# A change to the order of loads, conversions and first instructions in the attention stage of a fused attention, SwiGLU and top-1-expert kernel

## The chip, the cores and the metric

The kernel runs on one core of one Trainium2 chip. The metric is device time in microseconds (us) of one launch. Engines are named as in the profile: PE is TensorE's matmuls, PEld its weight loads, DVE is VectorE, ACT is ScalarE, POOL is GpSimd, SP is SyncE, which issues nearly all DMAs here. Each engine works through its own instructions in a fixed order and waits at any whose input or buffer isn't ready.

## What is computed

The reference, cut to its core (B=2, H=8, S=768, D=64; then 1536 tokens of 512, two feed-forward layers):

```python
scores = q @ k.T / 8 - slope[h] * dist      # local window n_local or first n_global keys, else -1e9
a = softmax(scores);  x = (a @ v) as [1536, 512]
xn = x / sqrt(mean(x*x) + 1e-6) * rms_g
x = (silu(xn @ w_gate) * (xn @ w_val)) @ w_out          # 1536 hidden columns, weights in float64
e = argmax(x @ r_gate);  out = gate * (relu(x @ w1[e]) @ w2[e])   # 8 experts
```

The SwiGLU weights arrive as float64, so each block of them is loaded raw (512 KB) and converted on the chip to a pair of rounded parts, high and low. Matmuls outside the first half of attention take such pairs too (high times high, high times low, low times high).

## The kernel before, in words

Attention is cut into 6 stages of 256 tokens and 4 pairs of heads: 24 groups g0 to g23, each with 2 units of 128 queries, so units u0 to u47. Groups 0 to 7 (`NRAWG = 8`) multiply queries and keys as they come. From g8 on, keys and queries are split into rounded parts first: ACT writes the high part of the keys (L519), DVE the low one (L522), then ACT and DVE do the same for the queries (L531, L532), and POOL copies pieces (L446). A unit is: scores on PE (L572 for raw groups, L586 for split ones), table added and row maximum on DVE (L590), exponential on ACT (L594), transposes on PE (L605), their copy on ACT (L613), values on PE (L634), and after a group's second unit a division on DVE (L641 to L643). After a stage's last group come its norm (L412 to L418) and four transposes per 128 tokens, whose result ACT and DVE take out of PSUM as a pair (L428, L429). From then on the first SwiGLU sweep of that stage (L801, L809 to L819, L838, L847) can run between the units.

SP loads keys, queries and values of a group in `load_pair`. Keys of group g are asked for when group g-2 is prepared, queries and values one group ahead. There are three key buffers and two query buffers (`NKN, NQN = 3, 2`), so a load also waits until the group that had the buffer has read it. A raw weight block goes through `load64` (L344) into one of three raw buffers (`NRAW = 3`), and `convert64` turns it into a pair: absolute value on ACT (L358), clamp, shift, sign and low bits on DVE (L361, L364, L367, L370), high part on ACT (L377), low part on DVE for the first four blocks and on POOL after that (L378).

The program is written in one order and a scheduler, which reckons each instruction's time, sets the final order on each engine. A helper, `behind(i, first)`, asks that instruction `i` stand behind `first` in that order; it adds no semaphore. The body counts events in `nun` (one at the start, one for each unit, one for each finished stage), and gives out the nine conversions of the first sweep (gate and value blocks 0, 1, 2, then three output blocks) by a list:

```python
    PREPS = [2, 4, 6, 8, 20, 22, 24, 27, 30]
            pin["load"] = key_load.get(10) if nun >= 12 else None
            while preps and nun > PREPS[9 - len(preps)]:
                preps.pop(0)()
```

`pin["load"]` is what a raw block's load must stand behind on SP: the key load of g10, once 12 events have passed. `pin["act"]` is the last exponential written so far, and a conversion's first ACT instruction stands behind it.

Before the body, the kernel reads `n_global` and `n_local`, makes tables from them on DVE and POOL (L275 to L292), halves them on ACT (L297), and works out a flag (L124 to L131) that every engine reads to choose between the fast and the dense body (L310, L1378). PE runs 24 dummy matmuls (`WARM0`, L181) ahead of its reading of the flag, 12 more at the body's start and two with each of the first 16 units.

Of the kernel before, what the change touches and what calls it, by code (L numbers as in the profile page):

```python
# [8 lines left out]
F32 = mybir.dt.float32  # L9
# [4 lines left out]
ACTF = mybir.ActivationFunctionType  # L14
ALU = mybir.AluOpType
# [4 lines left out]
P = 128  # L20
# [4 lines left out]
NP = H // 2  # L25
# [20 lines left out]
def kernel(  # L46
# [16 lines left out]
    nc = tc.nc  # L63
    slope = [2.0 ** (-(h + 1)) for h in range(H)]
# [11 lines left out]
    NDV = 512  # L76
    HP = 0
    NRAW = 3
    PREPS = [2, 4, 6, 8, 20, 22, 24, 27, 30]
    NA = 3  # L80
    MMA = "mm mm mm s s"
    MMB = "mm mm mm s s"
# [14 lines left out]
    TAILSEQ = "rrxrxxr"  # L97
    WARM3 = 6
    TAIL, TOFF = [0]*6, 0
    WARM0, WARM1, WARM2, WARMU = 24, 12, (2,), 16  # L100

    const = ctx.enter_context(tc.tile_pool(name="const", bufs=1))
    dram = ctx.enter_context(tc.tile_pool(name="dram", bufs=1, space=DRAM))
# [15 lines left out]
        out=nval, in0=nneg, scalar=4294967296.0, in1=nf[:, :, 0], op0=ALU.mult, op1=ALU.add  # L119
    )  # L120
    ng, nl = nval[:, 0:1], nval[:, 1:2]
# [6 lines left out]
    )  # L128
    nc.vector.tensor_tensor(out=flagf[:, 3:4], in0=flagf[:, 0:1], in1=flagf[:, 2:3], op=ALU.mult)
    flag = const.tile([1, 1], I32, name="flag")  # L130
    nc.vector.tensor_copy(flag, flagf[:, 3:4])  # L131


    gB = const.tile([P, DM], F32, name="gB")
# [16 lines left out]

    mhalf = const.tile([P, ST_MAX], F32, name="mhalf")
    nc.vector.memset(mhalf, -0.5)

    wz = const.tile([P, P], BF16, name="wz")
    nc.vector.memset(wz, 0.0)
# [12 lines left out]
    def behind(i, first):  # L169

        tc.add_manual_dep(
            i.ins, first.ins.name,
            mybir.DependencyInfo(mybir.DependencyClass.NoSync, mybir.DependencyReason.DATA), reason="order",
        )
# [26 lines left out]
    def is_raw(st, hp):  # L201
        return st * NP + hp < NRAWG

    last_load, key_load = [None], {}

    def load_pair(st, hp, kn, qn, vn, what="kqv"):
        b, t0, nt = STARTS[st] // TB, STARTS[st] % TB, SIZES[st]
        i0 = 0 if t0 else 1
        nk = nt + 1 - i0
        k0 = (t0 - 1 + i0) * P  # L210
        hd = slice(P * hp, P * (hp + 1))
        if is_raw(st, hp):
            if "k" in what:
                last_load[0] = nc.sync.dma_start(out=kn[:, 0:nk * P], in_=kT[b][hd, k0:k0 + nk * P])
            if "q" in what:
                nc.sync.dma_start(out=qn[:, 0:nt * P], in_=qT[b][hd, t0 * P:(t0 + nt) * P])
        else:
            for c, x, src in (("k", kn, kT[b][hd, k0:k0 + nk * P]), ("q", qn, qT[b][hd, t0 * P:(t0 + nt) * P])):
                if c not in what:
                    continue  # L220
                for r in range(2):
                    i = nc.sync.dma_start(
                        out=x[D * r:D * (r + 1), 0:2 * src.shape[1]].rearrange("d (j s) -> d j s", j=2),
                        in_=src.rearrange("(j d) s -> d j s", j=2),
                    )
                if c == "k":
                    last_load[0] = key_load[st * NP + hp] = i
        if "v" in what:
            nc.sync.dma_start(
                out=rows_of(vn)[:, i0:i0 + nk, 1:P + 1],  # L230
                in_=v[b, k0:k0 + nk * P, hd].rearrange("(t p) c -> p t c", p=P),
            )
        return kn, qn, vn
# [38 lines left out]
    tabG = const.tile([P, 256], F32, name="tabG")  # L272
    tab0 = const.tile([P, P], F32, name="tab0")
    gcol = const.tile([P, GW], F32, name="gcol")
    nc.vector.tensor_scalar(out=keep, in0=rel, scalar1=nl, scalar2=None, op0=ALU.is_lt)  # L275
    nc.vector.scalar_tensor_tensor(out=keep, in0=rel, scalar=0.0, in1=keep, op0=ALU.is_ge, op1=ALU.mult)
    nc.vector.tensor_tensor(out=rel, in0=rel, in1=keep, op=ALU.mult)
    nc.vector.tensor_scalar(out=keep, in0=keep, scalar1=-MASK, scalar2=MASK, op0=ALU.mult, op1=ALU.add)
# [33 lines left out]
    def body(is_fast):  # L312
# [122 lines left out]
        def fast_attention(pool):  # L435
# [12 lines left out]
            def prep(gi):  # L448
# [64 lines left out]
                src = kn[:, 0:2 * nk * P].rearrange("p (j t n) -> p j t n", j=2, t=nk)  # L513
                ks = kt[:, :, OW + i0:OW + nt + 1, :]
                hi_dve = HI[gi >= HIN]
                if hi_dve[0]:
                    nc.vector.tensor_copy(ks, src)
                else:
                    nc.scalar.activation(out=ks, in_=src, func=ACTF.Copy)  # L519
                lo_eng = (nc.vector, nc.gpsimd)  # L520
                kq = KQ0 if gi < KQN else KQ
                lo_eng[kq[0]].tensor_tensor(out=ks[D:P], in0=src[D:P], in1=ks[D:P].bitcast(F32), op=ALU.subtract)  # L522
# [3 lines left out]
                if hi_dve[1]:  # L526
                    nc.vector.tensor_scalar(
                        out=qhi, in0=srq, scalar1=0.125 / slope[2 * hp], scalar2=None, op0=ALU.mult
                    )
                else:  # L530
                    nc.scalar.activation(out=qhi, in_=srq, func=ACTF.Copy, scale=0.125 / slope[2 * hp])  # L531
                lo_eng[kq[1]].scalar_tensor_tensor(  # L532
                    out=qt[:, :, 1, 0:n], in0=srq, scalar=0.125 / slope[2 * hp], in1=qhi.bitcast(F32),
                    op0=ALU.mult, op1=ALU.subtract,
# [9 lines left out]
            units = [(g, t) for g in range(len(order)) for t in range(SIZES[order[g][0]])]  # L544

            def scores(g, t):
                st, t0, hp, qt, kt, vn, vx, mx = groups[g]
                if not is_raw(st, hp):
                    sb = ps("s", NS, "sp")
                    sp = [sb[:, 0:256], sb[:, 256:512]]  # L550
                else:
                    un = units.index((g, t))
                    mmb = is_raw(st, hp) and un % 2
                    sp = [ps(*(("mm", NMM) if mmb else ("s", NS)), "sp") for _ in range(2)]
                first = t0 + t == 0
                plain = t0 + t == 1
                n = P if first else 256
                tab = tabs[0 if first else 1 if plain else 2]
                pr = pool.tile([P, 2, 256], F32, tag="pr", bufs=NPR, name="pr")
                OW = ST_MAX  # L560
                raw_ = is_raw(st, hp)
                if raw_:
                    kn, kgr_ = kt
                    mm = warm(WARM2[un % len(WARM2)], into=sp) if un < WARMU else None
                    rows = [slice(D * j, D * (j + 1)) for j in range(2)]
                    if t0 == 0:
                        parts = [((0, n), kn[:, 0:n])]
                    else:
                        parts = [((0, GW), kgr_[:, hp, :]), ((GW, n), kn[:, t * P + GW:(t + 2) * P])]
                    for (c0, c1), keys in parts:  # L570
                        for o, r in zip(sp, rows):
                            last_, mm = mm, nc.tensor.matmul(  # L572
                                out=o[:, c0:c1], lhsT=qt[r, t * P:(t + 1) * P], rhs=keys[r], start=True, stop=True
                            )
                            if last_ is not None:
                                behind(mm, last_)
                for j, a in () if raw_ else ((0, 0), (0, 1), (1, 0), (1, 1)):
                    o = sp[j][:, 0:n]
                    if first:
                        rhs = kt[:, j, OW + 1, :]  # L580
                    elif plain:
                        rhs = kt[:, j, OW + t:OW + t + 2, :].rearrange("p t n -> p (t n)")
                    else:
                        rhs = kt[:, j, t:t + OW + 2:OW + 1, :]
                        o = o.rearrange("p (a n) -> p a n", a=2)
                    mm = nc.tensor.matmul(  # L586
                        out=o, lhsT=qt[:, j, a, t * P:(t + 1) * P], rhs=rhs, start=(a == 0), stop=(a == 1)
                    )
                for j in range(2):
                    nc.vector.tensor_tensor_reduce(  # L590
                        out=pr[:, j, 0:n], in0=sp[j][:, 0:n], in1=tab[j][:, 0:n], scale=-slope[2 * hp],
                        scalar=3.0e38, op0=ALU.add, op1=ALU.min, accum_out=mx[:, t, j:j + 1],
                    )
                    pin["act"] = nc.scalar.activation(  # L594
                        out=pr[:, j, 0:n], in_=pr[:, j, 0:n], func=ACTF.Exp, bias=mx[:, t, j:j + 1],
                        scale=-1.0,
                    )
                return pr, n
# [597 lines left out]
        nun = 0  # L1196
# [5 lines left out]
        while True:  # L1202
            with tc.high_priority(HP):
                ev = next(att, None)
            if ev is None:
                break
            if isinstance(ev, tuple):
                ready.append(ev[1])
            nun += 1
            if is_fast and nun == LATE:  # L1210
                late_loads()
            pin["load"] = key_load.get(10) if nun >= 12 else None
            while preps and nun > PREPS[9 - len(preps)]:
                preps.pop(0)()
            credit += MOE_RATE
            while True:
                if moe is None and ready:
                    st = ready.pop(0)
                    moe = moe_block(0, range(M0[st]), st, mpool, False)
                    credit = 0.0  # L1220
                if moe is None or credit <= 0:
                    break
                c = next(moe, None)
                if c is None:
                    moe = None
                    done += 1
                else:
                    credit -= c
# [197 lines left out]
```

## Time and profile before

| what | us |
|---|---|
| median of 3 runs | 648.56 |
| lowest, highest of them | 645.32, 649.33 |
| the profiled execution | 643.62 |
| its span, first to last instruction | 641.9 |
| around the span | 1.72 |

The span is what the trace shows; rows below are of that one execution, in us from its start. "Granted clock" is the share of TensorE's full clock (2.4 GHz) that the chip granted; 0.50 is the lower of its two levels, 1.2 GHz. In rows by stretch the columns are the stretch, its length, then busy us (and number of instructions) of PE, PEld, DVE, ACT and POOL, the granted clock, the share of the DMA engines and GB/s. Bracketed numbers in a row of the timeline are the engine's idle time just before, and what ended it.

### The profile page before, as it was taken

The page shows a single profiled execution, that of the slowest core. Times are in us where ns is not written, and L with a number is a line of the kernel's source. Part 1 is how long each engine was busy: PE and PEld are TensorE (multiplying, and loading weights), DVE is VectorE, ACT ScalarE, POOL GpSimd, SP SyncE. Part 2 cuts the span into 40 slices and gives each one's busy share as a digit, 9 for nine tenths or more (in the row PEclk, how much of TensorE's full clock was granted, in tenths as well). Part 3 has the DMA queues.
Part 4 walks back from the last instruction along what each step waited for, and adds up shares of the span by engine and source line. Part 5 has one row for each costly group of instructions (what it writes and reads, how often), then busy time and mean ns, then how long its engine had stood idle before and what let it go on. Part 6 is the DMA issues. An engine that isn't in the chain of part 4 may idle for free. (4 is left out here: it accounts for less than half of the span.)

```text
span 641.9 us, 11652 instructions
## 1 busy us (share of the span) xinstructions
PE 623.2 (97%) x4280; PEld 560.2 (87%) x4281; DVE 446.6 (70%) x1096; ACT 317.4 (49%) x623; POOL 179.5 (28%) x255
## 2 busy tenths in 40 slices
PE   8988989999999999999999999999999999999995
PEld 3667979999999999999999999997788998998994
DVE  3967989896599997775359998953576656556520
ACT  2867957797455543335522221242566556455420
POOL 4323434353121321221222533461701211011011
PEclk9998969999999999999999999999999999999998
DMA  7567556540044442221411020343777658465000
GB/s 220 150 188 182 168 158 186 154 98 28 1 117 146 132 138 93 66 67 66 132 66 66 1 67 34 89 159 100 272 259 249 222 206 266 148 227 181 5 29 32
DMA packets 56567, 82.98 MB, mean 129 GB/s; under 512 B 7983, under 2 KB 38703, under 8 KB 56496
## 3 DMA queue, kind: packets, MB, share of 16 engines
q1 hardware_dynamic: 53552, 74.75, 38.2%
q0 software_dynamic: 2944, 7.35, 3.4%
q8 instruction: 37, 0.61, 0.4%
q14 instruction: 34, 0.28, 0.1%
HBM read 75.75 MB, written 7.39 MB: 130 GB/s over the span
## 5 line engine op out<-in xcount | busy, mean ns | idle before, releaser
L801 PE MATMUL pg<-xn,gv 128*128 128x256 f32 x1728 | 226.2, 284 | 0.2 <-DVE hf L814 0.2
L801 PEld LDWEIGHTS pg<-xn,gv 128*128 128x128 f32 x1728 | 219.0, 190 | 7.0 <-DVE hf L814 0.7
L838 PE MATMUL po<-ow,hid 128*128 128x512 f32 x432 | 114.9, 398 | 0.1
L819 POOL TENSOR_TENSOR hid<-hf,hid 128x256 fp32r<-128x256 f32 x72 | 63.1, 878 | 166.6 <-ACT hid L818 166.5
L1049 PE MATMUL py<-ew,eh 128*128 128x512 f32 x384 | 91.1, 395 | 0.8 <-DVE eh L1116 0.4
L838 PEld LDWEIGHTS po<-ow,hid 128*128 128x128 f32 x432 | 76.1, 189 | 12.4 <-DVE hf L814 0.3
L1049 PEld LDWEIGHTS py<-ew,eh 128*128 128x128 f32 x384 | 71.3, 188 | 17.5 <-DVE eh L1116 0.8
L1071 PE MATMUL ph<-xs,ew 128*128 128x256 f32 x672 | 83.0, 283 | 0.0
L1071 PEld LDWEIGHTS ph<-xs,ew 128*128 128x128 f32 x672 | 81.6, 190 | 0.7
L818 ACT ACTIVATE hid<-hf 128x256 fp32r<-128x256 f32 x72 | 29.9, 415 | 84.9 <-DVE hf L814 84.9
L870 DVE CUSTOM_DVE_ANT_0 jk<-duo,rgb 128x512 bf16<-128x512 f32 x64 | 54.3, 848 | 0.5
L989 DVE TENSOR_TENSOR ew<-rawe,ew 128x1024 fp32r<-128x1024 f32 (+1 forms) x36 | 40.7, 1134 | 13.2 <-ACT ew L985 13.2
L1080 DVE SCALAR_TENSOR_TENSOR eh<-ph,eh 128x256 fp32r<-128x256 f32 x56 | 23.1, 422 | 37.3 <-ACT eh L1079 37.3
L809 ACT ACTIVATE th<-pg 128x256 f32<-128x256 f32 x72 | 27.2, 380 | 44.0 <-PE pg L801 41.6
L304 POOL DMA_INDIRECT out_dram<-yo,tk x14 | 14.6, 1040 | 120.3 <-ACT yo L1057 92.6
L989 DVE TENSOR_TENSOR ew<-duo,ew 128x1024 fp32r<-128x1024 f32 x28 | 34.1, 1223 | 17.9 <-ACT ew L985 17.0
L594 ACT ACTIVATE pr<-pr,mx 128x256 f32<-128x256 f32 (+1 forms) x96 | 41.9, 484 | 9.3 <-DVE mx L590 9.1
L985 ACT ACTIVATE ew<-rawe 128x1024 fp32r<-128x1024 f32 x36 | 38.0, 1060 | 10.5 <-PE pg L801 4.7
L810 DVE SCALAR_TENSOR_TENSOR th<-th,pg 128x256 f32<-128x256 f32 x72 | 29.6, 413 | 15.5 <-ACT th L809 15.3
L1079 ACT ACTIVATE eh<-ph 128x256 fp32r<-128x256 f32 x56 | 21.2, 385 | 38.8 <-PE ph L1071 38.7
L985 ACT ACTIVATE ew<-duo 128x1024 fp32r<-128x1024 f32 x28 | 29.4, 1060 | 19.4 <-PE py L1049 19.4
L847 DVE TENSOR_TENSOR duo<-duo,po 128x512 f32<-128x512 f32 x36 | 23.3, 681 | 22.2 <-PE po L838 22.1
(183 smaller groups left out, 890.0 us busy)
## 6 DMA issues: line engine op xcount, KB each, us to landing
rawe<-in_moe_w_dram SPq DMA_DIRECT2D x36, 512.0 KB, 4.6
duo<-in_moe_w_dram SPq DMA_DIRECT2D x28, 512.0 KB, 4.3
raw<-in_moe_w_gate_dram SPq DMA_DIRECT2D x12, 512.0 KB, 4.4
raw<-in_moe_w_val_dram SPq DMA_DIRECT2D x12, 512.0 KB, 4.3
raw<-in_moe_w_out_dram SPq DMA_DIRECT2D x12, 512.0 KB, 3.6
kn<-in_k_dram SPq DMA_DIRECT2D x28, 192.0 KB, 3.5
qn<-in_q_dram SPq DMA_DIRECT2D x36, 128.0 KB, 3.2
vn<-in_v_dram SPq DMA_DIRECT2D x16, 192.0 KB, 3.1
```

What stands on the lines that cost most here:

```text
L594: pin["act"] = nc.scalar.activation(out=pr[:, j, 0:n], in_=pr[:, j, 0:n], func=ACTF.Exp, bias=mx[:, t, j:j + 1], scale=-1.0,)
L801: nc.tensor.matmul(out=pg[:, 0:n_], lhsT=gv[:, i, a, kk, :], rhs=x[st][:, kk, :], start=(n == 0), stop=(n == 3 * KD - 1),)
L809: pin["th"] = nc.scalar.activation(out=th, in_=pss[0][:, 0:n_], func=ACTF.Tanh, scale=0.5)
L810: nc.vector.scalar_tensor_tensor(out=th, in0=th, scalar=1.0, in1=pss[0][:, 0:n_], op0=ALU.add, op1=ALU.mult)
L818: nc.scalar.activation(out=hh[:, 0], in_=hf, func=ACTF.Copy)
L819: nc.gpsimd.tensor_tensor(out=hh[:, 1], in0=hf, in1=hh[:, 0].bitcast(F32), op=ALU.subtract)
L838: nc.tensor.matmul(out=po, lhsT=hid[mi][:, a, t * P:(t + 1) * P], rhs=ow[:, c, :], start=(mi == 0 and n == 0), stop=(mi == len(ms) - 1 and ...
L870: nc.vector.tensor_tensor_reduce(out=jk, in0=part[i0 + t], in1=rgb[e // 4][:, e % 4, :], scale=1.0, scalar=0.0, op0=ALU.mult, op1=ALU.add, ...
L985: cp = nc.scalar.activation(out=t[:, 0], in_=raw, func=ACTF.Copy)
L989: nc.vector.tensor_tensor(out=t[:, 1, 0:nd], in0=raw[:, 0:nd], in1=t[:, 0, 0:nd].bitcast(F32), op=ALU.subtract)
L1049: last_mm["py"] = nc.tensor.matmul(out=py, lhsT=hid(m, a, j), rhs=w2t[m // 2][:, c, (m % 2) * DM:(m % 2 + 1) * DM], start=(n == 0), stop=( ...
L1071: nc.tensor.matmul(out=ph[:, 0:CAP], lhsT=w1t[kk][:, a, m * P:(m + 1) * P], rhs=x[:, kk, :], start=(n == 0), stop=(n == 3 * KD - 1),)
```

## The change

- The conversions of gate block 2, value block 2 and output block 0 are given out at events 14, 16 and 18 in place of 20, 22 and 24; those of output blocks 1 and 2 at 26 and 29 in place of 27 and 30.
- Raw weight loads from event 12 on must stand behind the query load of g7, in place of the key load of g10. The key load of g10 must stand behind the query load of g8.
- For g8 and g9 the ACT instructions that write the high parts of keys and queries must stand behind the last exponential of the unit before (`late`, `pin["prev"]`).
- The first table instruction on DVE (L275) must stand behind the flag.
- A one-column exponential is put near the program's start on ACT. `WARM0` goes from 24 to 20.

```diff
-    PREPS = [2, 4, 6, 8, 20, 22, 24, 27, 30]
+    PREPS = [2, 4, 6, 8, 14, 16, 18, 26, 29]
-    WARM0, WARM1, WARM2, WARMU = 24, 12, (2,), 16
+    WARM0, WARM1, WARM2, WARMU = 20, 12, (2,), 16
-    nc.vector.tensor_copy(flag, flagf[:, 3:4])
+    flagged = nc.vector.tensor_copy(flag, flagf[:, 3:4])
+    first_exp = const.tile([P, 1], F32, name="first_exp")
+    nc.scalar.activation(out=first_exp, in_=mhalf[:, 0:1], func=ACTF.Exp)
-    last_load, key_load = [None], {}
+    last_load, key_load, q_load = [None], {}, {}
@@ load_pair
-                nc.sync.dma_start(out=qn[:, 0:nt * P], in_=qT[b][hd, t0 * P:(t0 + nt) * P])
+                q_load[st * NP + hp] = nc.sync.dma_start(out=qn[:, 0:nt * P], in_=qT[b][hd, t0 * P:(t0 + nt) * P])
                 for r in range(2):
+                    g = st * NP + hp
                     i = nc.sync.dma_start(
                         out=x[D * r:D * (r + 1), 0:2 * src.shape[1]].rearrange("d (j s) -> d j s", j=2),
                         in_=src.rearrange("(j d) s -> d j s", j=2),
                     )
+                    if c == "k" and 10 <= g <= 10:
+                        behind(i, q_load[g - 2])
                 if c == "k":
                     last_load[0] = key_load[st * NP + hp] = i
+                else:
+                    q_load[st * NP + hp] = i
@@ tables
-    nc.vector.tensor_scalar(out=keep, in0=rel, scalar1=nl, scalar2=None, op0=ALU.is_lt)
+    behind(nc.vector.tensor_scalar(out=keep, in0=rel, scalar1=nl, scalar2=None, op0=ALU.is_lt), flagged)
@@ prep
+                def late(i):
+                    if gi < 10:
+                        behind(i, pin["prev"])
-                    nc.scalar.activation(out=ks, in_=src, func=ACTF.Copy)
+                    late(nc.scalar.activation(out=ks, in_=src, func=ACTF.Copy))
-                    nc.scalar.activation(out=qhi, in_=srq, func=ACTF.Copy, scale=0.125 / slope[2 * hp])
+                    late(nc.scalar.activation(out=qhi, in_=srq, func=ACTF.Copy, scale=0.125 / slope[2 * hp]))
@@ scores
+                pin["prev"] = pin["act"]
@@ body's loop
-            pin["load"] = key_load.get(10) if nun >= 12 else None
+            pin["load"] = q_load.get(7) if nun >= 12 else None
```

## Rows read from the trace of the kernel before

**Rows 1.** Busy time of each engine, granted clock and DMA, by stretch.
```profile
44.00:60.00 16.00, 11.46 (x74) 10.37 (x75) 11.24 (x35) 10.44 (x24) 5.56 (x13) 0.79 0.90 219
46.90:53.70 6.80, 4.86 (x22) 4.24 (x21) 4.99 (x18) 3.49 (x8) 1.01 (x2) 0.50 1.11 234
60.00:84.00 24.00, 22.28 (x190) 21.60 (x188) 23.56 (x65) 19.86 (x45) 11.41 (x21) 1.00 0.61 177
80.00:96.00 16.00, 13.44 (x70) 12.34 (x70) 13.19 (x39) 9.19 (x21) 5.78 (x11) 0.68 0.58 159
84.40:94.70 10.30, 9.67 (x42) 9.18 (x43) 8.01 (x24) 6.70 (x16) 3.17 (x5) 0.50 0.42 120
...
160.00:641.90 481.90, 473.11 (x3196) 433.01 (x3194) 320.69 (x686) 203.44 (x371) 117.94 (x117) 1.00 0.37 121
```

**Rows 2.** What SP issues around g7 to g10, in order of time.
```profile
32.36 0.54 SPq L216 DMA_DIRECT2D qn<-in_q_dram  x1
...
37.51 2.93 SPq L222 DMA_DIRECT2D kn<-in_k_dram  x4
40.49 0.60 SPq L344 DMA_DIRECT2D raw<-in_moe_w_gate_dram  x1
...
41.68 1.26 SPq L222 DMA_DIRECT2D qn<-in_q_dram  x2
42.98 0.59 SPq L344 DMA_DIRECT2D raw<-in_moe_w_out_dram  x1
```

**Rows 3.** DMA issues of 40 to 44 us: KB each, us from issue to landing.
```profile
raw<-in_moe_w_gate_dram SPq DMA_DIRECT2D x1, 512.0 KB, 4.8
...
raw<-in_moe_w_out_dram SPq DMA_DIRECT2D x1, 512.0 KB, 8.3
...
qn<-in_q_dram SPq DMA_DIRECT2D x2, 128.0 KB, 6.9
```

**Rows 4.** The timeline around the first loss: start, us, engine, line.
```profile
39.19 0.89 ACT L594 ACTIVATE pr<-pr,mx 128x256 f32<-128x256 f32 x2
...
42.74 0.84 ACT L519 ACTIVATE kt<-kn 128x768 fp32r<-128x768 f32 x1 [2.66 <-DMA kn<-in_k_dram]
...
49.28 0.63 ACT L531 ACTIVATE qt<-qn 128x512 fp32r<-128x512 f32 x1 [2.08 <-DMA qn<-in_q_dram]
...
50.05 2.28 PE L586 MATMUL sp<-kt,qt 128*128 128x256 f32 x8 [1.43 <-ACT qt L531]
```

**Rows 5.** The conversions' instructions up to 160 us: ns min/median/max, first and last start.
```profile
L361 DVE TENSOR_SCALAR cv<-cv x11: 394/421/1324, 18.1 to 108.3; 128x512 f32<-128x512 f32 x11
L364 DVE TENSOR_SCALAR cv<-cv x11: 410/427/628, 18.6 to 108.8; 128x512 uint32<-128x512 uint32 x11
L367 DVE SCALAR_TENSOR_TENSOR cv<-raw,cv x11: 675/689/1649, 19.3 to 109.4; 128x512 uint32<-128x512 uint32 x11
L370 DVE SCALAR_TENSOR_TENSOR cv<-raw,cv x11: 679/694/1686, 20.8 to 113.4; 128x512 uint32<-128x512 uint32 x11
...
L378 POOL TENSOR_TENSOR gv<-cv,gv x2: 1272/1282/1292, 72.7 to 78.2; 128x512 fp32r<-128x512 f32 x2
```

**Rows 6.** The timeline around the second loss, and the conversion before it.
```profile
63.98 0.67 ACT L358 ACTIVATE cv<-raw 128x512 f32<-128x512 f32 x1
...
77.28 0.62 ACT L428 ACTIVATE xn<-trx 128x512 fp32r<-128x512 f32 x1
...
82.37 0.68 DVE L429 TENSOR_TENSOR xn<-trx,xn 128x512 fp32r<-128x512 f32 x1
...
83.10 0.66 PE L605 MATMUL pp<-ident,pr 128*128 128x128 f32 x4 [1.72 <-DVE xn L429]
```

**Rows 7.** The timeline of the start.
```profile
5.91 2.50 PEld L181 LDWEIGHTS <-wz 128*128 128x128 bf16 x12 [0.28 <-issue]
...
7.15 0.13 DVE L131 CAST flag<-flagf 1x1 int32<-1x1 f32 x1
...
8.40 1.28 ACT L297 ACT_TABLE_LOAD   x1 [8.27 <-DVE tabG L288]
```

## The prediction

> **What bounds the kernel now.** I read the busy times by stretch first. After attention the kernel is bound by PE: from 160 us to the end PE is busy 473.11 of 481.90 us at a granted clock of 1.00, with DVE at 320.69 and ACT at 203.44 [rows 1]. The same matmuls have to run whatever the attention stage does, so a microsecond that PE loses before 160 us is a microsecond at the end, and one given back there is given back at the end, as long as PE finds work to take up. The change touches the first 100 us only, so the question is what PE loses there.
>
> There are two losses. From 44 to 60 us PE is busy 11.46 of 16.00 us, idle 4.54; and from 46.9 to 53.7 us the granted clock is 0.50, TensorE's 1.2 GHz level, while PE is busy 4.86 us, which would have taken half of that at 2.4 GHz: 2.43 more [rows 1]. First loss: 6.97 us. From 80 to 96 us PE is busy 13.44 of 16.00, idle 2.56, and from 84.4 to 94.7 us the clock is 0.50 with PE busy 9.67 us, so 4.84 more [rows 1]. Second loss: 7.40 us. In both the clock fell after PE had stood idle in pieces.
>
> The order of SP's issues and the timeline then tell what each waited for. In the first, g8's queries are issued at 41.68, behind the raw gate block of 40.49 and its value block [rows 2], and they take 6.9 us to land [rows 3]; ACT waits for them until 49.28 and PE's first scores of the split groups start at 50.05 [rows 4]. Ahead of that, ACT has g9's key rounding in its order before the exponentials of g7; it waits for g9's keys until 42.74 [rows 4], and DVE, which has the low part of the same keys next, holds back the row maxima of g7's units with it. In the second, ACT has a transposed stage-0 tile ready at 77.28 + 0.62 = 77.90, but DVE takes its low part out of PSUM only at 82.37, so that PE's transposes start at 83.10 for want of the bank [rows 6]. DVE is 4.47 us late there, and it is full: 23.56 of 24.00 us between 60 and 84 [rows 1].
>
> **The change part by part.**
>
> *The start.* Four dummy matmuls fewer: twelve weight loads took 2.50 us [rows 7], 0.21 each, so PE comes to its reading of the flag 4 x 0.21 = 0.83 us earlier. The flag is written at 7.15 + 0.13 = 7.28 us [rows 7], and with the table instructions behind it it comes earlier still, so PE would not wait for it. The table load on ACT (1.28 us at 8.40 [rows 7]) moves into time in which ACT has nothing; the halved tables follow at once when their inputs are there. The tables themselves get later by what little the flag's chain now takes alone. SP is not helped: its twelve loads ahead of the body stay. Bounds: 0 (the first units wait for data) to -0.83; I take -0.6, near the upper row, since PE, ACT and DVE all come earlier and only SP doesn't.
>
> *SP's order.* The three raw loads (gate 2, value 2, output 0) may now go right behind g7's queries of 32.36, five to ten us before they went [rows 2]. Their raw buffers are free by then, since the first four blocks are converted in the 20s and low 30s. Three loads are 1.5 MB; at the 4.8 us that one took in a crowd [rows 3] they would be in by about 39 us. g8's queries then have g9's keys ahead of them and no weights; with g10's keys put behind them, they go out near 39 instead of 41.68 and should land in half the 6.9 us, so near 42.5, in place of 49.28.
>
> *Rounded parts pinned.* g8's key rounding now stands behind u13's exponential, which ends at 39.19 + 0.89 = 40.08 [rows 4]; with 0.84 on ACT, about as much again on DVE and a copy on POOL its keys are whole near 42.5, no later than its queries. g9's stands behind u15's, so it can no longer hold DVE back at 42.74. PE's first split scores should start near 43.5 in place of 50.05.
>
> *Conversions.* One costs DVE 0.421 + 0.427 + 0.689 + 0.694 = 2.23 us [rows 5]. Gate 2 was converted from 63.98 on [rows 6], in the stretch where DVE is full; six events earlier, three conversions (6.7 us of DVE) come to lie between about 40 and 58 us. DVE has 16.00 - 11.24 = 4.76 us idle from 44 to 60 [rows 1], but much of that idle time is the stall itself. So the first stretch becomes bound by DVE, and of its 6.97 us I count half as won: -3.5 (bounds: 0 when DVE fills all of it, -6.97). In the second stretch 6.7 us of work leave, more than the 4.47 by which DVE was late. The idle time should go and most of the low clock; other DVE work may slip in, and the output blocks come one event earlier. Of 7.40 I take -4.5 (bounds 0 and -7.40).
>
> *What it costs.* The conversions' low parts run on POOL, 1.28 us each, and beside the first of these the DVE instruction L370 took its longest, 1.686 in place of 0.694 us [rows 5]. Three of these move into a stretch bound by DVE: 3 x 0.99 = 3.0 at most, 0 if they fall beside instructions that don't mind; I take +1.0, as DVE's time there is only partly the bound. A page of the Trainium skill (SBUF — State Buffer, section "SBUF: two separate sides") goes further: VectorE and GpSimd share a port pair that one holds for a whole instruction while the other is shut out. By that rule the three cost up to 3 x 1.28 = 3.8, an estimate, and the sum would be 1 us worse or so; the 0.99 in the row is the measured size and I keep to it.
>
> **The sum.** -0.6 - 3.5 - 4.5 + 1.0 = -7.6 us. The profiled execution took 643.62 us (its span of 641.9 and 1.72 around it), so it would be 636.0. That execution was faster than all three timed runs; on their median, 648.56, the same difference gives 641.0, which I predict.
>
> **The rivals.**
>
> *The stalls move and DVE decides.* If the conversions take all that DVE wins in the first stretch, or the scheduler leaves the raw loads behind g9's keys for want of a free buffer (then the change doesn't do what it says), the first loss stays: 0; the second loses its idle time but the clock still falls, -2.56; start -0.6: -3.2, so 645.4. For it: DVE at 23.56 of 24.00 is as tight as PE. Against: between 44 and 60 us DVE, ACT and PE are all idle at times, so a wait and no engine is the bound there.
>
> *Both losses go whole.* -6.97 - 7.40 - 0.6 = -15.0: 633.6. For it: both start from a wait that the change names. Against: 6.7 us of DVE work are not taken away, only moved.
>
> *Slower: ACT waits for raw weights.* A conversion's first ACT instruction stands behind the last exponential written, so it now sits between the exponentials of u13 to u19. If the raw block hasn't landed when ACT comes to it, ACT stops with all exponentials behind it, then DVE and PE. It decides once the raw loads go out at 38 us or later beside g9's keys and g8's queries: they then take up to 8.3 us [rows 3] and land at 46. The first loss is then had twice, +6.97, the second stays, and the three POOL subtractions add 3.0: with the start's -0.6 it is +9.4, so 658.0. For it: SP works in order, and one wait for a key buffer ahead of the weights is enough. Against: the weights need only stand behind the load of 32.36, and SP stands waiting at 37.51 for a buffer, which is just the kind of gap that a scheduler fills.
>
> **How the numbers follow.** Forecast 0.57 (own range 637.0 to 645.0), stalls move 0.22, both go 0.10, slower 0.11. A difference of 1% here, 6.5 us, is about what a measurement of this kernel can tell from no change; the bounds are 642.1 and 655.0. Of the forecast's 0.57 some 0.43 lies under 642.1, with the 0.10 of both losses gone: faster 0.53. The other 0.14 and the 0.22: same 0.36. Slower 0.11. The range reaches from 633.5, both losses gone, to 650.5, where half of what was won has been given back and more, and leaves out the slow case.
>
> **What would show each step.** Raw gate and value loads on SP between 33 and 37 us; g8's queries landing before 44; PE's first L586 near 43.5; the third and fourth conversion steps of gate 2 on DVE before 50 us instead of near 70; DVE's low part L429 following ACT's within 2 us around 75 to 85; granted clock 1.00 from 60 to 100 us; the first scores 0.6 to 0.8 us earlier. The prediction is wrong if ACT shows waits for a raw block's DMA, if a stretch at 0.50 as long as before stands anywhere under 100 us, or if PE's idle time up to 160 us has not shrunk by some 5 us.

## The result, and the profile after

The changed kernel takes 641.99 us (median of 6 runs, 641.30 to 643.07) beside 648.23 for the kernel before in the same session (6 runs, 645.32 to 649.33): the medians are 6.2 us or 1.0% apart, and the ratio is 0.9918, with a 95% interval of 0.9891 to 0.9945. In a second session of ten runs it took 642.56 beside 647.39, ratio 0.9924 [0.9895, 0.9953]. Ratios and fits leave out slow runs, which take over 1.5% longer than the fastest of their kernel, such as the 647.74 us of the conversions given out as before; medians and ranges hold every run. The forecast was 641.0. The total came out as worked; most of the reasons behind it did not, and the rest of this document is about that.

The profiled execution after took 641.56 us (span 639.9, 1.66 around it). That is only 2.06 less than the profiled one of before, 643.62. The medians differ by three times as much, because the profiled execution of before was 4.6 us under its own median.

First the busy times by stretch of the kernel after, columns as in [rows 1].

```profile
44.00:60.00 16.00, 11.97 (x70) 11.16 (x70) 15.04 (x41) 11.57 (x24) 8.76 (x14) 0.66 0.70 192
...
49.20:62.90 13.70, 10.59 (x49) 10.21 (x50) 12.71 (x30) 9.03 (x18) 5.69 (x10) 0.50 0.61 187
60.00:84.00 24.00, 24.00 (x201) 24.00 (x199) 21.23 (x62) 19.33 (x44) 10.29 (x20) 0.94 0.50 147
80.00:96.00 16.00, 16.00 (x132) 15.39 (x130) 14.74 (x47) 13.61 (x33) 5.67 (x11) 1.00 0.61 165
...
160.00:639.90 479.90, 470.17 (x3164) 432.17 (x3162) 319.19 (x683) 202.17 (x369) 118.73 (x116) 0.99 0.37 122
```

Against [rows 1]: the second loss has gone whole. PE is busy 16.00 of 16.00 us from 80 to 96, at a clock of 1.00, and DVE no longer fills 60 to 84 us (21.23 of 24.00). The first loss has grown. From 44 to 60 us PE is idle 4.03 us in place of 4.54, but the low clock now lasts 13.7 us, with PE busy 10.59, half of which is 5.30: together 9.33 in place of 6.97. In the 5.20 us before the clock fell, from 44.00 to 49.20, PE had been idle 0.92. DVE is busy 15.04 of the 16.00 us from 44 to 60, where it had been busy 11.24.

What SP issues around g7 to g10, after (start, us, queue, line, output and input):

```profile
32.06 0.39 SPq L352 DMA_DIRECT2D raw<-in_moe_w_gate_dram  x1
32.55 0.45 SPq L352 DMA_DIRECT2D raw<-in_moe_w_val_dram  x1
33.10 0.44 SPq L352 DMA_DIRECT2D raw<-in_moe_w_out_dram  x1
36.48 1.26 SPq L226 DMA_DIRECT2D kn<-in_k_dram  x2
37.83 2.05 SPq L226 DMA_DIRECT2D qn<-in_q_dram  x2
```

This answers to [rows 2]: the raw blocks go out 8 to 10 us earlier, and g8's queries at 37.83 in place of 41.68. The timeline of the kernel after, at the places of [rows 4] and [rows 6] (columns as there; brackets: idle time before, and what ended it):

```profile
42.73 0.63 ACT L544 ACTIVATE qt<-qn 128x512 fp32r<-128x512 f32 x1 [1.91 <-DMA qn<-in_q_dram]
...
44.58 1.19 PE L600 MATMUL sp<-kt,qt 128*128 128x256 f32 x8
...
47.48 1.27 POOL L386 TENSOR_TENSOR gv<-cv,gv 128x512 fp32r<-128x512 f32 x1
...
47.68 2.49 DVE L426 SCALAR_TENSOR_TENSOR duo<-duo,ry,gB 128x512 f32<-128x512 f32 x2
...
50.09 0.63 DVE L369 TENSOR_SCALAR cv<-cv 128x512 f32<-128x512 f32 x1
...
51.30 0.95 DVE L535 TENSOR_TENSOR kt<-kn,kt 64x768 fp32r<-64x768 f32 x1
...
52.41 0.94 POOL L454 TENSOR_SCALAR kt<-kt 128x384 fp32r<-128x384 f32 x1 [1.97 <-DVE kt L535]
...
53.40 0.58 PE L600 MATMUL sp<-kt,qt 128*128 128x256 f32 x1 [2.87 <-POOL kt L454]
...
78.02 0.58 ACT L436 ACTIVATE xn<-trx 128x512 fp32r<-128x512 f32 x1
...
78.63 0.69 DVE L437 TENSOR_TENSOR xn<-trx,xn 128x512 fp32r<-128x512 f32 x1
```

ACT gets g8's queries at 42.73 (before: 49.28) and PE starts the split scores at 44.58 (before: 50.05). The new wait is the chain that ends at 53.40. g9's low key part stands on DVE behind the two halves of the norm (47.68 to 50.17) and the steps of a conversion, and comes at 51.30. POOL's copy waits for it, and PE stands 2.87 us for POOL. In the second stretch DVE follows ACT at once: 78.02 + 0.58 = 78.60, and L437 starts at 78.63, where L429 had been 4.47 us late.

The start, after, beside [rows 7]; the last row is of before:

```profile
0.84 1.28 ACT L156 ACT_TABLE_LOAD   x1 [0.70 <-PEq L1417]
...
6.29 0.14 DVE L131 CAST flag<-flagf 1x1 int32<-1x1 f32 x1
...
8.88 0.49 PE L586 MATMUL sp<-duo 64*128 64x128 f32 x4
...
10.29 0.49 PE L572 MATMUL sp<-duo 64*128 64x128 f32 x4
```

The table load has moved into idle time, the flag comes at 6.29 in place of 7.15, and the first scores start at 8.88 in place of 10.29.

### The profile page after: what moved, and what is told of

It reads as the page before. It is cut to its first block, busy times and chain, and to the rows that moved or that the text cites. A ratio compares the mean times of both kernels' runs of the same rounds, so it can differ in the third digit from the quotient of the medians.

```text
span 639.9 us, 11649 instructions
## 1 busy us (share of the span) xinstructions
PE 620.7 (97%) x4276; PEld 561.3 (88%) x4277; DVE 445.8 (70%) x1096; ACT 318.2 (50%) x624; POOL 181.3 (28%) x255
## 5 line engine op out<-in xcount | busy, mean ns | idle before, releaser
L852 PE MATMUL po<-ow,hid 128*128 128x512 f32 x432 | 113.1, 394 | 1.4 <-POOL ow L386 1.4
L852 PEld LDWEIGHTS po<-ow,hid 128*128 128x128 f32 x432 | 76.2, 189 | 13.7 <-POOL ow L386 1.9
```

The lines of the kernel that those rows point to most:

```text
L852: nc.tensor.matmul(out=po, lhsT=hid[mi][:, a, t * P:(t + 1) * P], rhs=ow[:, c, :], start=(mi == 0 and n == 0), stop=(mi == len(ms) - 1 and ...
```

## The experiments

Two theories. The first is the prediction's: the kernel gained because g8's queries and keys come earlier and because the conversions leave the stretch in which DVE made PE wait; then PE's idle time before 160 us falls. The rival: idle time stays about what it was, and what changes is how long TensorE stands at its lower level, which differs also from run to run of one kernel.

**What the kernel before does by itself** (no edit).

> The kernel before itself, unchanged. The changed kernel's profiled execution was only 2.06 us shorter than that of before (641.56 against 643.62), while the medians differ by 6.24 (641.99 against 648.23). Theory 1: the profiled execution of before was a lucky one; another profile takes 646 to 649 us and shows the extra 3 to 5 us as PE idle time or half-clock time before 100 us. Rival: the extra time lies outside the span (more than 1.72 us around it), and the span stays near 642.

Measured: 647.58 us (641.55 to 650.26, 12 runs), 0.9992 [0.9961, 1.0023]. Each run comes with its mean granted clock, here as a share of the full clock. Over these twelve, time and clock go together (correlation -0.92, a fitted 0.53 us for each 0.001 of clock). In 27 other runs of the kernel before in the same session they do so again (-0.91, 0.47 us), from 642.55 us at .988 to 650.49 at .971, and in 27 and 33 of the two later sessions (-0.80, 0.40; -0.85, 0.45). The size is what arithmetic allows: 0.001 of 640 us is 1.28 us at half clock, in which PE would lose 0.64 if it were always busy. This execution took 648.77 us, near the usual for the kernel before. Its stretches:

```profile
44.00:66.00 22.00, 16.79 (x94) 15.56 (x94) 13.27 (x43) 13.56 (x30) 5.85 (x14) 0.69 0.78 190
47.90:54.80 6.90, 4.82 (x21) 4.32 (x21) 4.65 (x18) 3.27 (x7) 0.63 (x2) 0.51 1.10 220
58.20:65.00 6.80, 6.80 (x34) 6.80 (x33) 2.63 (x10) 3.33 (x7) 1.82 (x5) 0.50 0.52 150
80.00:100.00 20.00, 17.54 (x102) 16.11 (x102) 17.04 (x47) 11.74 (x27) 8.29 (x13) 0.74 0.61 164
88.90:99.10 10.20, 9.73 (x42) 9.24 (x43) 7.85 (x22) 6.60 (x16) 3.17 (x5) 0.50 0.44 125
```

The same code has a third stretch at 0.50, from 58.2 us, that the first profile did not show. PE is busy without a gap in it; in the 3.40 us before it PE had been idle 1.20. It costs half of 6.80, 3.40 us, and with the others of this run (half of 4.82 and of 9.73) 10.68. So the profile that the prediction was worked from had one low stretch fewer than this one; its mean clock was .983, and the median of these twelve runs is .979. A page of the Trainium skill (TensorE: Matmul & The Clock Gate, section 'Part 1: The HAM clock gate (the "warmup" mystery)') says of the ramp at a kernel's start that the number of slow matmuls varies between runs of one kernel, and that the ramp costs under 1% of a typical span. The stretches here come in the middle of a kernel: they vary between runs too, and they cost more, 10.68 of 647.0 us or 1.7%.

**The kernel after, again** (no edit).

> The changed kernel itself, on the chip and beside the runs of before that the other three share, to compare it with its versions at the old events. Theory 2: 641 to 643, mean clock 0.984 to 0.990 in all runs; a profile shows one long stretch at 0.50 between 45 and 65 us and none between 80 and 96. Rival (its first result was luck of the clock): 644 to 648 with a clock of 0.980.

Measured: 642.56 us (639.81 to 643.14, 10 runs), 0.9924 [0.9895, 0.9953], median mean clock .987 where the kernel before had .979 beside it. The difference of .008, at 0.40 to 0.53 us for each .001, would be 3.2 to 4.2 us of the 4.83 between the two medians. Two stretches of this execution:

```profile
52.10:62.30 10.20, 9.43 (x45) 9.43 (x46) 9.31 (x22) 5.96 (x12) 4.34 (x8) 0.50 0.61 181
80.00:96.00 16.00, 16.00 (x130) 15.47 (x130) 14.74 (x46) 13.61 (x32) 6.07 (x13) 1.00 0.62 169
```

The pattern repeats: one low stretch after 50 us, nothing from 80 to 96. Now 0 to 160 us in five executions, one fence each: before (span 641.9), before again (647.0), after (639.9), after again (638.0), and the next experiment's (636.3).

```profile
0.00:160.00 160.00, 150.06 (x1087) 127.21 (x1089) 125.93 (x410) 113.98 (x252) 61.57 (x138) 0.95 0.57 154
```

```profile
0.00:160.00 160.00, 149.04 (x1046) 125.88 (x1047) 123.63 (x404) 111.58 (x247) 60.96 (x135) 0.93 0.57 154
```

```profile
0.00:160.00 160.00, 150.50 (x1113) 129.12 (x1115) 126.64 (x414) 116.02 (x255) 62.61 (x139) 0.96 0.55 154
```

```profile
0.00:160.00 160.00, 150.67 (x1118) 129.62 (x1120) 126.01 (x414) 116.69 (x256) 62.34 (x139) 0.97 0.56 154
```

```profile
0.00:160.00 160.00, 149.27 (x1119) 125.64 (x1121) 128.75 (x414) 115.65 (x256) 63.77 (x139) 1.00 0.56 154
```

PE's busy time is the same within 1.6 us, so its idle time is too: 9.9, 11.0, 9.5, 9.3 and 10.7 us. What differs is how many matmuls fit into it, 1087, 1046, 1113, 1118 and 1119, and they follow the clock, .95, .93, .96, .97 and 1.00, and the spans. Idle time and half of what PE does at 0.50 come together to 17.2, 21.6, 14.8, 14.0 and 10.7 us before 160 us. Beside the first of them the other four stand at +4.4, -2.4, -3.2 and -6.5, and their spans at +5.1, -2.0, -3.9 and -5.6. This speaks for the rival.

**The conversions given out as before.**

```diff
-    PREPS = [2, 4, 6, 8, 14, 16, 18, 26, 29]
+    PREPS = [2, 4, 6, 8, 20, 22, 24, 27, 30]
```

> The changed kernel with the conversions at the old events (20, 22, 24, 27, 30). Theory 1 (the conversions' DVE work fills 60 to 84 us and makes the second loss, 7.4 us): the second loss is back, the first one shrinks since DVE is freer there, total 644 to 647. Rival (the waits for loads and roundings made all of the losses, the conversions' place is nothing): 642, or below, and no loss between 80 and 96 us.

Measured: 639.37 us (637.16 to 647.74, 6 runs), 0.9882 [0.9832, 0.9932]. Four of the runs have a clock of .992 to .997 and take 637.2 to 640.6; one at .987 takes 641.96, and one at .979 takes 647.74. Stretches and two rows of the timeline:

```profile
44.00:60.00 16.00, 12.57 (x102) 11.39 (x101) 14.07 (x46) 13.47 (x29) 7.49 (x15) 1.00 0.66 165
...
70.00:80.00 10.00, 7.71 (x65) 7.15 (x65) 9.88 (x25) 5.91 (x14) 5.68 (x9) 1.00 0.65 176
...
80.00:96.00 16.00, 15.24 (x114) 13.77 (x114) 15.80 (x46) 13.84 (x31) 7.13 (x12) 1.00 0.58 160
```

```profile
74.31 0.60 ACT L436 ACTIVATE xn<-trx 128x512 fp32r<-128x512 f32 x1
...
79.21 0.67 DVE L437 TENSOR_TENSOR xn<-trx,xn 128x512 fp32r<-128x512 f32 x1
```

DVE's lateness is back: ACT is done at 74.91 and DVE follows at 79.21, 4.3 us later, with DVE busy 9.88 of 10.00 us and PE idle 2.29. So this much was read rightly: conversions at events 20 to 24 make DVE late at that place. But the price of the place is 2.3 us of idle time and no more when the clock does not fall after it. In this execution it falls nowhere before the last microseconds of the program, and the kernel without the new conversion events is not slower than the one with them (the two intervals overlap).

**The conversions alone**: the kernel before with that one list changed to the new one.

> The kernel before with the new events for the conversions alone. The raw loads still stand behind g10's keys. Theory 1 with its slow rival's mechanism: the absolute value on ACT now stands among the exponentials of u13 to u19 while its raw block lands at 46 us or later, so ACT waits for a raw block's DMA and the time is 650 or more. Rival (the conversions' place alone frees DVE and wins the second loss): 642 to 645, no wait of ACT for raw.

Measured: 642.92 us (640.65 to 650.59), 0.9936 [0.9906, 0.9967], about 4.5 us less than before. Two rows of SP and one stretch:

```profile
24.51 0.37 SPq L344 DMA_DIRECT2D raw<-in_moe_w_gate_dram  x1
...
41.60 0.60 SPq L344 DMA_DIRECT2D raw<-in_moe_w_val_dram  x1
```

```profile
80.00:96.00 16.00, 16.00 (x132) 15.40 (x131) 12.26 (x48) 12.39 (x29) 4.55 (x10) 1.00 0.56 149
```

PE is full from 80 to 96 us here too. Counting all profiles of this study: the six kernels with the new events (after in two profiles) never show a clock under 1.00 between 80 and 100 us; of the six with the old events, before (both times), the start alone and the last one below show a stretch at 0.50 there, three do not. So with the new events the second low stretch is gone in every profile, and alone they bring most of what the whole change brings. They are not the only thing that goes with its absence: all three profiles with the old events and SP's old rules show it, and of the four with the old events and SP's new rules three do not. The slow rival's wait did not come, but this run tests it only in part: the gate block is given out before g10's key load has been written, has no load to stand behind and goes out at 24.51.

**The start alone**: the kernel before with 20 dummies, the early exponential and the flag first.

```diff
-    WARM0, WARM1, WARM2, WARMU = 24, 12, (2,), 16
+    WARM0, WARM1, WARM2, WARMU = 20, 12, (2,), 16
@@ start, cut
+    nc.scalar.activation(out=first_exp, in_=mhalf[:, 0:1], func=ACTF.Exp)
@@ tables, cut
-    nc.vector.tensor_scalar(out=keep, in0=rel, scalar1=nl, scalar2=None, op0=ALU.is_lt)
+    behind(nc.vector.tensor_scalar(out=keep, in0=rel, scalar1=nl, scalar2=None, op0=ALU.is_lt), flagged)
```

> The kernel before with the change's start alone: 20 dummy matmuls, the early exponential, the flag ahead of the tables. Theory 1: first scores 0.6 to 0.8 us earlier, total -0.6 us against the kernel before, both losses still there. Rival: the start shifts the whole order of the attention stage and is worth several us by itself, -4 or more.

Measured: 645.57 us (640.5 to 650.12), 0.9966 [0.9936, 0.9996]: 1.9 us less, with an interval that just leaves out no change. First scores at 9.26 in place of 10.29. A small gain is there; its size is not better known than the interval, 0.3 to 4 us, in which the 0.6 of the forecast lies too.

**SP's two rules as before.**

```diff
-            pin["load"] = q_load.get(7) if nun >= 12 else None
+            pin["load"] = key_load.get(10) if nun >= 12 else None
@@ load_pair
-                    if c == "k" and 10 <= g <= 10:
-                        behind(i, q_load[g - 2])
```

> The changed kernel with SP's two rules as before: raw loads behind g10's keys, g10's keys not behind g8's queries. Theory 1 (the order of the raw loads carries the early conversions): ACT waits for a raw block or for g8's queries, the first split scores start near 50 us again, total 648 to 655. Rival (DVE sets the first stretch and loads have slack): 642 and first split scores before 46 us.

Measured: 644.46 us (642.83 to 647.53), 0.9962 [0.9937, 0.9986]. Two rows of SP and PE's first split scores:

```profile
23.30 0.37 SPq L350 DMA_DIRECT2D raw<-in_moe_w_gate_dram  x1
...
37.71 1.24 SPq L226 DMA_DIRECT2D qn<-in_q_dram  x2
...
44.33 1.20 PE L598 MATMUL sp<-kt,qt 128*128 128x256 f32 x8
```

The scores start as early as with the new rules (44.58). But the old rules do not bring the old order back: as with the conversions alone, the gate block slips out early, at 23.30, and g8's queries go at 37.71 with no weights just ahead of them. So with the new events SP's new rules are not needed for the early scores; what the old order itself costs this run does not tell. In the total the rules are worth some 2.5 us by the medians (after took 4.83 less than before, this kernel 2.29, in another session), with intervals that overlap.

**The pins taken out** (`late` does nothing).

```diff
                 def late(i):
-                    if gi < 10:
-                        behind(i, pin["prev"])
+                    return
```

> The changed kernel without the pinned roundings of g8 and g9. Theory 1: the pin is worth the wait of ACT and DVE for g9's keys only when these land late; now that no weights stand ahead of them it is worth little, total 641 to 644. Rival (the pin is what lets the raw groups' row maxima run): g7's row maxima wait for g9's keys again, 646 to 650.

Measured: 641.99 us (639.92 to 644.16, 6 runs), 0.9924 [0.9897, 0.9951]. Timeline:

```profile
44.08 0.84 ACT L531 ACTIVATE kt<-kn 128x768 fp32r<-128x768 f32 x1 [3.96 <-DMA kn<-in_k_dram]
...
50.52 1.84 PE L599 MATMUL sp<-kt,qt 128*128 128x256 f32 x7
```

Without the pins ACT waits 3.96 us for g9's keys with all that stands behind it, and the split scores start at 50.52, 6 us later than after. The total is the same as with them. So in this order it is the pins that bring the scores forward, and the earlier start is worth nothing that can be measured.

**SP's order alone, without and with the start.** The first is the kernel before with the SP rules; the second has the new start too (old conversion events, no pins in both).

> The kernel before with SP's two rules alone (raw loads behind g7's queries, g10's keys behind g8's queries). Prediction's step: g8's queries land near 42.5 in place of 49.3 and the first split scores start 5 to 7 us earlier; total 641 to 645. Rival (loads had slack, some other wait is next): first split scores at 48 us or later, 646 to 648.

> The changed kernel with the conversions at the old events and no pinned roundings: SP's order and the start alone. Theory 2: the pins decide nothing by themselves; what counts is whether PE stands idle long enough near 45 to 60 us for the clock to fall, total 639 to 645 with the time following the clock. Rival (with the old events the pins hold DVE free, as the prediction had it): g7's row maxima wait for g9's keys, 646 to 648.

Measured: 645.09 us, 0.998 [0.9951, 1.001], and 645.31 us, 0.9971 [0.9943, 0.9999]. The timeline of the first:

```profile
42.23 0.84 ACT L528 ACTIVATE kt<-kn 128x768 fp32r<-128x768 f32 x1 [2.41 <-DMA kn<-in_k_dram]
...
48.87 2.05 PE L596 MATMUL sp<-kt,qt 128*128 128x256 f32 x8
```

Its stretch from 80 to 96 us:

```profile
80.00:96.00 16.00, 13.89 (x109) 12.74 (x108) 15.36 (x45) 11.76 (x27) 7.42 (x13) 1.00 0.70 183
```

SP's rules alone leave the split scores at 48.87 and bring nothing that can be told from no change. PE is idle 2.11 us from 80 to 96, nearly as long as the 2.56 of [rows 1], but the clock does not fall. Adding the start to them adds nothing, though alone it gave 1.9. The parts do not add up: start -1.9, conversions -4.5, SP -2.3, all of it -4.8 to -6.2, all but the conversions -8.1. Each edit lets the scheduler order the whole attention stage anew, so a kernel with one part taken out differs in more than that part. Nor does the clock alone set the time of a version: these two have a median clock of .99, above the .987 of the kernel after in the same session, and take 2.5 and 2.8 us longer. In the profile of the second, PE is idle 13.1 us before 160 us, where the five above have 9.3 to 11.0.

**One pin fewer**: only g8 pinned, to take away PE's wait at 53.40.

```diff
-                    if gi < 10:
+                    if gi < 9:
```

> The changed kernel with g8 alone pinned, g9's roundings free. In the changed kernel g9's keys wait on DVE until 51.3 us and PE idles 2.87 us for them. Theory 1 (the first stretch is bound by the order on DVE): g9's low part comes earlier, PE's idle time near 51 us shrinks, total 638 to 641. Rival (it is bound by DVE's amount of work): another wait takes its place, 641 to 644.

Measured: 645.87 us (642.49 to 648.49), 0.998 [0.9953, 1.0006]. PE no longer waits for POOL's copy of g9's keys. Its stretch:

```profile
44.00:68.00 24.00, 21.44 (x102) 20.16 (x101) 18.08 (x53) 16.32 (x34) 9.41 (x17) 0.58 0.65 185
```

PE is idle 2.56 of 24.00 us, less than the 4.03 of the kernel after in this place, but the granted clock is 0.58 over the whole of it (two low stretches, some 20 us at 0.50), and the gain is gone; this execution took 648.42 us, 2.5 over its kernel's median. Idle time and the clock's loss did not move together.

**Dummies to hold the clock**: the kernel after with six dummy matmuls ahead of the scores of each of units u16 to u21.

```diff
+                un_ = units.index((g, t))
@@ scores of split groups, cut
+                if not raw_ and un_ < 22:
+                    warm(6, into=(sb, sb))
```

> The changed kernel with six more dummy matmuls ahead of the scores of each of units 16 to 21. In the changed kernel PE idles from 50.5 to 53.4 us and the clock is 0.50 from 49.2 to 62.9 us with PE busy nearly all of the last 8 us. Theory 1 (half of that stretch is lost to the clock, 4 to 5 us): the clock stays at 1.00 and the total falls by 2 to 5 us, less what the dummies take. Rival (DVE is the bound there and the clock costs nothing): no gain, or 1 to 2 us slower.

Measured: 643.81 us (642.36 to 646.31), 0.9956 [0.9934, 0.9978], mean clock .993 to .999 in every run. One stretch, and one of the six groups of dummies:

```profile
44.00:64.00 20.00, 17.64 (x111) 12.85 (x110) 18.20 (x46) 14.46 (x30) 7.93 (x14) 0.91 0.72 192
```

```profile
47.35 1.47 PE L184 MATMUL sp<-wz 128*128 128x512 bf16 x6
```

The clock did what the theory says: it is high and nearly constant, with one stretch of 3.4 us at 0.50 in this profile. The spread of the times, 4.0 us, is no smaller than that of the kernel after (3.3). Five of the groups take 1.46 to 1.47 us, and the one in the low stretch takes 2.72: 10.1 us of PE. Before 160 us PE's idle time is 7.4 us in place of 9.5 and the half lost at 0.50 is 1.7 in place of 5.3, so 5.7 us were given back. The dummies show that the clock can be held; they do not pay.

**Fewer dummies in the order that kept its clock by itself**: the old conversion events with two dummies in the same units. The line of the diff is beside the kernel with six; the list of events is the old one.

```diff
-                    warm(6, into=(sb, sb))
+                    warm(2, into=(sb, sb))
```

> The changed kernel with the conversions at the old events and two dummy matmuls ahead of the scores of each of units 16 to 21 (12 in all, 0.21 us each at full clock, 2.6 us). Theory 2 (after the first runs: PE's idle time before 160 us is about 7 us in every version, and the time goes with how long the clock stands at 0.50): mean clock 0.992 or more in nearly all runs, the spread of times shrinks, median 637 to 641. Rival (DVE's amount of work bounds the stage): the dummies change nothing but add up to 2.6 us, spread as wide as without them, 640 to 643.

Measured: 644.70 us (640.31 to 648.99), 0.995 [0.9918, 0.9982], clock .989. A miss: the clock is lower than without the dummies, with two stretches of 3.4 us at 0.50 under 100 us, and PE is idle 2.16 us from 100 to 112, with DVE full, where it was idle 1.37 without them:

```profile
100.00:112.00 12.00, 9.84 (x77) 9.02 (x76) 11.87 (x32) 9.31 (x23) 6.44 (x8) 1.00 1.03 244
```

No kernel of this study is shown to beat the one after. The one with the old conversion events has the lowest median, 639.37, but its interval holds the ratio of after.

## Why the prediction was right, and where its steps failed

The total on the medians was right, and the profiles say how. Against a more usual execution of before (the one of 648.77 us), the kernel after loses less in these places: from 44 to 66 us before has 5.21 idle and half of 4.82 and 6.80, 11.0, and after has 4.03 and 5.30, 9.3: -1.7. From 80 to 100 us before has 2.46 idle and half of 9.73, 7.3, and after 1.44 with a clock of 1.00: -5.9. The first scores come 1.9 us earlier (10.8 there, 8.88). In the other direction, after has a stretch of 3.41 us at 0.50 from 448.6 us that this profile of before lacks, with PE busy throughout: half of it, 1.7. The sum is -7.8, and the executions differ by 7.2. Against the profile that the prediction was made from, which had one low stretch fewer, only 2.06 us are left where -7.6 was worked out: on the profiles the sum was wrong by 5.5. So the step "on their median, 648.56, the same difference gives 641.0" had no ground, since a profile 4.6 us under its median does not hold the losses of a usual run; it happened to make up for the terms that failed, and that the total came out is luck to that extent.

*The start*: forecast -0.6. The first scores came 1.41 us earlier, and the start alone measured -1.9 [0.9936, 0.9996]. Sign right; the size is not known well enough to call the term wrong. The dummies' price alone (0.83) was no upper bound for the first scores: the flag and the halved tables came earlier as well. Nor is their time the start's alone: with the old conversion events and the same start they come at 9.79.

*SP's order*: the rules did what they say. The raw loads went out right behind g7's queries, g8's queries landed for ACT at 42.73 (forecast near 42.5) and the scores started at 44.58 (forecast near 43.5). The attribution failed: with SP's new order and no pins the scores start at 48.87 or 50.52, with SP's rules undone and the pins kept at 44.33, and with the conversions alone at 46.51; in the last two the gate block was out early as well. Pins with the weights still ahead of g8's queries were not run.

*Rounded parts pinned*: they keep ACT and DVE from waiting on g9's keys, as said. What failed is the reading before it, that the first loss is what PE waits for g8's queries and for ACT and DVE behind g9's keys. Without the pins these waits are back, the scores start 6 us later, and the total is the same.

*First loss*: forecast -3.5 of 6.97, measured +2.4 between the two profiles. This is the term that failed. I put the bound at zero "when DVE fills all of it", and DVE did fill it (15.04 of 16.00), but that was no bound: with DVE full, PE's idle time shrank by only 0.5 us, and the low clock, for which the step had no term that could grow, cost 5.30 in place of 2.43. That the fuller DVE is why it lasted longer is argued from this profile and not shown.

*Second loss*: forecast -4.5 of 7.40; all 7.40 went between 80 and 96 us, with 1.44 of idle time new at 97 us. DVE's lateness is gone, as the step said. The low clock there is gone in every profile with the new events, but the step's reason for it is not borne out: with the old events DVE was late again by 4.3 us and the clock did not fall, and SP's new rules alone went without the low stretch too.

*POOL beside DVE*: forecast +1.0. The longest norm instruction on DVE beside a POOL subtraction (47.48 to 48.75) shows in the group of that line, from 40 to 80 us:

```profile
L426 DVE SCALAR_TENSOR_TENSOR duo<-duo,ry,gB x4: 751/862/1616, 47.7 to 72.1; 128x512 f32<-128x512 f32 x4
```

It is the first of the two of 47.68 and took 1.616 in place of the median 0.862 us: 0.75 lost, near the 0.99 of the row I used, and on the chain that ends in PE's wait at 53.40. By the page of the Trainium skill named in the prediction (SBUF — State Buffer, section "SBUF: two separate sides") the pair of ports would be shut to DVE until POOL ends at 48.75, 1.07 us; the measured loss is less. No run took this cost away by itself.

*The rivals.* That the stalls move and DVE decides is what happened from 44 to 60 us, but its price was wrong, since the second loss went whole. The slow case did not come: SP issued the raw loads at 32 to 33 us, well ahead of the 38 at which it would have begun.

*The tests I set.* Two of those that were to prove me wrong came true: a low stretch longer than before stands under 100 us (13.7 us, from 49.2), and PE's idle time up to 160 us shrank by 0.4 us and not by 5. The third did not: ACT's one wait for a raw block up to 160 us is 0.69 us at 25.78, for one of the first four blocks, whose events the change left as they were. The terms were wrong in opposite directions (first loss by +5.9, second by -2.9, the start's first scores by -0.8), and the gaps that came anew, 1.44 at 97 us and the 1.7 at 448.6, stood in none. What stays open is why the order with the old conversion events and the pins keeps its clock in most runs (median .994) and the kernel after does not (.987); no run here settles it.

## What to carry to other kernels

Before two versions that differ by 1% are compared, list the mean granted clock of each run beside its time, and take the profile whose time is nearest to the median: here .001 of clock was 0.40 to 0.53 us, and the profiled execution was 4.6 us better than usual. A wait removed from an in-order engine is worth what PE's idle time and its clock show after it, not the microseconds by which the waiting instruction moves; here, with another engine nearly full in that stretch, the gaps moved. Moving work off a stretch in which an engine is full brought 4.5 us by itself here, with that engine busy 18.00 of 22.00 us where the work went (the conversions alone, 44 to 66 us), so read its busy time in both places. What it brings where the new place is full was not measured by itself.

## What was not expected of the hardware

In 27 runs one program, in order and inputs the same, took between 642.55 and 650.49 us on one core, with mean granted clocks from .988 to .971. A stretch at 0.50 of 6.8 us can appear in one execution, with PE busy in all of it, and be absent in the next. Idle time did not tell how long the clock stays low: 2.56 us idle went with some 20 us at 0.50 (one pin fewer), 3.43 us with none (old conversion events). And queries of 128 KB needed 6.9 us from issue to landing when 512 KB raw blocks had gone out just ahead of them [rows 3], and ACT read them 7.6 us after their issue; issued at 37.83, 4 us behind the last raw block, they were there for ACT 4.9 us later.
